# One PSUM bank per feed-forward slice, and a new order of all steps, in an RWKV-7 and SwiGLU kernel

## The chip, the cores and the metric

The kernel runs on one core of a Trainium2 chip. The metric is device time in microseconds (us) of one execution. Before the change three runs took 1074.79, 1076.04 and 1078.73 us; the median is 1076.04 us. A core has five engines with queues of their own: TensorE (PE, with its weight loads shown apart as PEld), VectorE (DVE), ScalarE (ACT), GpSimd (POOL) and SyncE (SP, which issues DMAs here). An engine takes its instructions strictly in the order of its queue, and waits between engines are made with semaphores.

## What is computed

The first half is the RWKV-7 recurrence for 4 batches of 8 heads, 768 steps, head size 40. The second half is a SwiGLU feed-forward block on the 3072 x 320 result.

```python
for t in range(S):
    y[:, :, t] = einsum('bhd,bhde->bhe', r_t, state)
    Sa = einsum('bhde,bhe->bhd', state, a_t)
    state = state * w_t[:, :, None, :] - einsum('bhd,bhe->bhde', Sa, b_t)
    state = state + einsum('bhd,bhe->bhde', v_t, k_t)
...
xn = x / sqrt(mean(x * x) + 1e-6) * rms_g      # x: (3072, 320)
g = xn @ w_gate                                # (320, 1536)
out = (g * sigmoid(g) * (xn @ w_val)) @ w_out  # (1536, 320)
```

## The kernel before, in words

**Stages.** The sequence is cut into 24 chunks of 32 steps. For every chunk, `front` loads the inputs and builds the matrices of the chunk (transposes, "gramk" products, their scaled copies), `inverse` inverts a triangular matrix by small DVE steps (`early_inverse` for the first four chunks), and `main` carries the state over, forms the chunk's output and normalises it into `xg`. After every second chunk `feed(g)` (L941) runs the feed-forward block on 256 token columns: 12 groups in all. In the first group the weights are also narrowed (L975) and written to DRAM as twelve slices `sW[f]`, which later groups load again.

**A feed-forward pair.** `feed` takes the twelve slices of 128 hidden units two at a time, so a pair has the slices e = 0 and e = 1, and there are 72 pairs. A pair takes one PSUM room `hh` of 128 x 2 x 512 f32 (L952), that is two banks. Its steps are:

- `h64` (L959): four matmuls with 64 rows, for the last 64 of the 320 model dimensions; gate and value of both slices,
- `h` for each e (L962): four matmuls of 128 x 256 columns, two for the gate and two for the value,
- `act` (L964): ACT computes the SiLU of the gate into `sg`,
- `tt` (L965): DVE multiplies the value with it into `hT`,
- `out` (L966): two matmuls of 128 x 320 add `hT` times the output weights into `po`.

Before the change, bank 0 of the room holds the two gates and bank 1 the two values, so either slice lies half in each bank (L953).

**Rooms and pairs.** Eight PSUM banks are used: `po` has two, and three tiles `ps` of two banks each, called pairs, hold everything else. A room (transposes, products, levels, feed-forward pairs: 499 in all) is given one of the three pairs by the string `PAIRS`.

**Order.** No loop decides in which order the engines work. `Plan.add` records every step with what it reads and writes, and `Plan.issue` then emits all 6028 recorded steps in the order that the string `ORDER` gives (each number is an offset from the first step not yet emitted; "-" emits a warm-up matmul into `po`, L1017, 151 of them). Semaphore waits are not in that string. They are derived by the framework as the steps are emitted, from the tiles which each step touches.

The level step of `main` (L882 to L885) and the step `down` (L887 to L895), which also shares a room between several users, come up in the prediction: a room `yl` (L914) takes three levels, two in bank 0 and one in bank 1, and DVE adds each of them into `y`.

Of the kernel before, what the change touches and what calls it, by code (L numbers as in the profile page):

```python
# [17 lines left out]
P = 128  # L18
# [15 lines left out]
85 84 76 83 58 78 73 86 74 59 60 75 5 89 61 88 53 77 80 4 43 6 201 7 87 90 44 8 334 62 9 - - - - - - - - 93 10 18 79  # L34
11 12 214 557 13 213 567 14 15 94 566 210 16 17 95 558 108 200 - - - 97 96 19 335 20 21 2 209 22 23 98 25 199 568 26
100 578 202 24 101 107 569 111 57 - - - - - 102 106 124 589 27 122 112 392 109 103 52 119 113 104 54 577 155 125 110
204 105 120 - - - - - - 114 203 117 121 559 211 598 118 46 131 129 132 45 562 560 212 597 563 588 561 394 123 115 136
586 384 133 134 - - - - - 126 130 116 47 564 3 145 383 135 336 128 137 48 144 143 141 587 219 142 51 570 127 565 146
138 337 55 573 1005 216 579 281 393 220 582 608 571 390 234 379 239 607 572 583 580 380 251 574 222 38 221 609 575 581
42 - - - - - - - - 223 82 226 339 91 64 227 338 39 81 139 224 263 576 238 153 56 249 247 590 206 584 228 382 237 591  # L40
272 593 40 233 232 585 381 154 148 594 33 140 205 229 592 389 235 250 28 248 - - 325 236 32 245 36 230 147 260 282 391
246 259 150 35 34 326 595 0 36 270 155 214 148 242 243 62 605 598 230 - 239 40 616 599 601 628 64 49 91 600 602 30 48
626 1135 28 257 603 29 241 68 150 255 65 0 1347 194 0 194 84 173 0 - - - 182 540 200 0 557 184 1 186 935 542 540 0 506
515 527 257 513 300 0 111 97 110 61 112 96 51 439 458 122 50 243 480 0 244 0 58 255 242 0 259 709 104 120 246 708 247
456 470 258 488 719 0 256 470 457 242 0 716 265 487 104 0 268 0 0 265 473 0 262 277 0 273 0 236 0 260 0 269 0 461 241
- - - - - - - 237 242 0 0 278 242 243 252 0 252 0 0 89 0 99 246 0 97 0 230 94 440 0 230 94 440 231 - - - - - - - - -
240 441 244 0 0 468 440 451 255 0 42 468 269 469 258 215 440 239 204 0 0 257 253 203 93 449 92 212 0 235 - - - - - - -
- 246 0 437 0 262 0 246 247 436 245 464 470 258 259 469 260 244 - - 255 471 465 468 466 0 215 466 269 256 445 697 255
478 686 93 94 264 95 687 270 96 266 97 0 97 470 695 2 98 99 3 100 471 101 473 1 102 0 468 99 470 100 471 101 441 102
103 258 104 105 260 106 - - - - - - - - - - - 0 504 106 107 473 108 0 108 502 0 108 109 469 110 111 0 0 0 0 0 - - 13 0  # L50
374 16 146 143 14 147 142 15 13 355 - - - 25 386 358 0 358 386 388 16 387 389 25 390 79 17 391 28 70 147 355 191 69
356 80 148 149 26 359 0 28 2 29 149 0 149 150 29 0 149 31 185 391 23 32 390 29 150 356 151 186 33 389 0 151 29 387 152
27 40 187 153 154 155 156 33 157 158 159 160 161 34 162 36 163 164 37 165 41 391 38 42 392 39 394 561 166 395 393 552
0 42 548 395 209 0 560 165 42 395 548 210 43 428 211 427 557 44 - - - 565 166 558 45 167 549 168 0 566 168 739 565 567
738 571 169 579 - - 45 728 572 0 124 139 0 535 682 0 535 545 140 578 536 141 0 547 545 546 543 578 0 558 554 567 0 519
- - - - - - 517 377 696 378 380 381 695 518 120 685 135 526 - - - - - - 522 686 379 527 382 136 530 383 554 529 121 -
- 141 540 123 523 565 539 122 537 142 125 538 124 524 - - - - 145 525 148 534 149 152 154 551 535 147 555 - - 157 146
# [3 lines left out]
607 367 478 34 568 - - 35 830 594 36 567 820 38 - 476 37 571 366 570 0 605 356 433 434 435 436 120 437 0 317 318 319  # L61
320 441 321 322 323 324 355 456 458 459 442 4 357 325 457 326 327 328 443 0 443 328 329 330 331 357 0 35 331 3 0 37
450 359 3 36 358 331 332 357 333 356 0 462 448 330 461 464 331 332 468 364 447 463 31 467 476 458 333 365 334 335 0
425 439 441 302 426 436 0 6 439 2 0 435 332 2 436 443 444 0 448 332 442 334 443 333 340 449 0 297 329 342 32 330 - 3
33 341 334 0 332 331 0 332 293 441 295 333 0 438 0 436 333 336 295 337 309 438 338 1 375 342 310 365 374 515 27 292 0
362 292 26 28 44 339 29 34 27 32 338 0 646 29 34 336 647 32 0 439 64 315 647 339 440 634 441 63 340 0 287 413 606 312
313 607 623 12 314 615 414 0 410 310 411 603 619 27 412 475 413 620 414 415 621 416 311 633 28 417 812 418 312 625 - -
- - 476 313 419 420 421 822 258 314 422 423 0 810 423 625 637 477 2 0 819 2 257 0 420 421 645 310 422 0 - - - - - 310
422 3 313 32 630 311 423 33 643 424 641 631 312 0 0 637 20 635 420 647 613 21 421 611 648 819 23 38 22 422 809 423 39
659 24 3 612 36 818 424 651 25 808 621 425 59 660 426 249 427 58 0 427 3 25 428 249 4 28 47 0 - 614 428 429 28 430 431  # L70
0 26 25 614 617 484 31 27 627 0 458 590 400 600 401 0 12 582 32 401 33 583 25 0 579 30 21 - - - - - - - - - 588 29 591
22 453 397 428 398 605 23 0 23 429 24 609 0 590 24 397 588 602 1 604 398 601 429 430 399 2 427 0 584 - - - - - - - - -
- - - - - 4 397 0 25 397 4 0 393 394 28 21 23 27 395 598 24 22 424 607 0 35 395 37 396 24 2 424 47 397 398 38 399 400
# [4 lines left out]
976 716 416 663 729 634 977 562 563 717 713 986 665 564 565 566 975 567 401 568 714 569 985 570 571 967 572 723 722 -  # L78
0 403 726 402 572 401 573 0 726 738 736 573 739 574 664 575 737 576 577 3 723 751 578 579 760 580 747 581 582 633 583
4 584 0 584 585 634 586 636 587 635 588 734 633 0 746 588 - - - - - 403 757 589 722 590 3 404 591 592 593 594 595 596  # L80
# [290 lines left out]
def kernel(  # L371
# [36 lines left out]
    DM = H * D  # L408
# [9 lines left out]
    GT = CG * P  # L418
# [74 lines left out]
    def pe(kind, steps, more=[]):  # L493
        def issue(at):
            for s in steps:
                s[3](at)
        plan.add("PE", kind, issue, [s[0] for s in steps] + more, [x for s in steps for x in s[1:3]])
# [58 lines left out]
    for m in range(4):  # L556
        e = eye[m * BH:(m + 1) * BH]
# [492 lines left out]
```

## Time and profile before

| what | us |
|---|---|
| runs | 1074.79, 1076.04, 1078.73 |
| span of the profiled execution | 1078.2 |
| PE busy | 1010.2 |
| DVE busy | 834.2 |
| ACT busy | 462.2 |
| POOL busy | 309.0 |

The results give no time for the profiled execution beside its span; the span is 2.2 us over the median of the runs and 0.5 us under the slowest run. The profile lists for each engine how long it was busy and, for groups of equal instructions, how long they took together, how long one took, and how long the engine sat idle right before them and what ended that wait. PE writes each f32 matmul as two records, so a group of 1152 records is 576 matmuls.

### The profile page before, as it was taken

How to read it: one execution, taken by the hardware profiler on the slowest of the kernel's cores; microseconds unless marked ns; L12 is line 12 of the kernel's file. 1: busy time of each engine (PE TensorE's matmuls, PEld its weight loads, DVE VectorE, ACT ScalarE, POOL GpSimd, SP SyncE). 2: the span in 40 equal slices, each digit the busy share in tenths (PEclk: the TensorE clock that was granted, in tenths of full speed). 3: DMA queues.
4: the chain of work that ended last, by engine and by line, in shares of the span. 5: the costliest groups of instructions: out<-in, count | busy, mean ns of one | idle time of the engine just before them, and what ended most of it. 6: DMA issues, size and time to landing. Idle time of an engine off the chain costs nothing. (4 is left out here: it accounts for less than half of the span.)

```text
span 1078.2 us, 53465 instructions
## 1 busy us (share of the span) xinstructions
PE 1010.2 (94%) x23406; PEld 828.3 (77%) x23406; DVE 834.2 (77%) x2861; ACT 462.2 (43%) x1043; POOL 309.0 (29%) x554
## 2 busy tenths in 40 slices
PE   6767899999999999999999999998999999999998
PEld 6766778777888787877788778887777887887776
DVE  7887879876868888887897888887788889797420
ACT  6845756643543433532443434433344344342211
POOL 9714404120532223241331331331332331200000
PEclk9778999999999999999999999999999999999999
DMA  9965448766564364574465654665545553744242
GB/s 180 196 155 123 73 106 220 213 127 177 124 142 122 99 150 116 144 145 120 96 152 133 146 126 112 142 142 123 126 106 110 134 150 90 162 109 123 77 140 86
DMA packets 172456, 143.34 MB, mean 133 GB/s; under 512 B 125504, under 2 KB 143872, under 8 KB 172224
## 3 DMA queue, kind: packets, MB, share of 16 engines
q1 hardware_dynamic: 153856, 116.96, 42.4%
q0 software_dynamic: 16192, 22.64, 12.2%
q8 instruction: 184, 3.01, 1.2%
q10 hardware_dynamic: 2176, 0.33, 0.2%
q14 instruction: 48, 0.39, 0.1%
HBM read 123.86 MB, written 15.99 MB: 130 GB/s over the span
## 5 line engine op out<-in xcount | busy, mean ns | idle before, releaser
L488 PE MATMUL ps<-xg,wf 128*128 128x256 f32 (+1 forms) x1728 | 355.2, 392 | 4.7 <-DVE xg L446 1.1
L488 PEld LDWEIGHTS ps<-xg,wf 128*128 128x128 f32 (+1 forms) x1728 | 261.6, 189 | 60.4 <-issue 16.9
L488 PE MATMUL po<-wf,hT 128*128 128x320 f32 x576 | 180.1, 445 | 0.1
L446 DVE TENSOR_TENSOR tmp<-Yi,M 128x60 f32<-128x60 f32 (+24 forms) x620 | 129.5, 209 | 19.7 <-DMA M<-sB 6.9
L446 DVE TENSOR_TENSOR Yi<-Yi,tmp 128x60 f32<-128x60 f32 (+24 forms) x620 | 130.2, 210 | 12.7 <-DVE ss L446 0.2
L466 ACT ACTIVATE sg<-ps 128x256 f32<-128x256 f32 x144 | 52.4, 383 | 192.4 <-PE ps L488 182.7
L488 PEld LDWEIGHTS po<-wf,hT 128*128 128x128 f32 x576 | 102.6, 191 | 34.0 <-issue 1.7
L485 POOL DMA_DIRECT2D VU<-in_v_dram x92 | 53.6, 587 | 234.2 <-PE ps L488 157.0
L446 DVE TENSOR_TENSOR hT<-ps,sg 128x256 f32<-128x256 f32 x144 | 59.0, 419 | 62.4 <-ACT sg L466 55.9
L469 ACT COPY KN<-ps 128x640 f32<-128x640 f32 x96 | 66.2, 691 | 76.6 <-PE ps L491 27.9
L488 PEld LDWEIGHTS ps<-Ab,K 40*64 40x64 f32 x4608 | 78.3, 139 | 26.4 <-issue 8.5
L446 DVE TENSOR_TENSOR K<-K,T 128x512 f32<-128x512 f32 (+1 forms) x192 | 93.3, 495 | 4.2 <-ACT K L469 2.1
L488 PE MATMUL ps<-Ab,K 40*64 40x56 f32 x4608 | 88.0, 225 | 8.8 <-ACT K L469 3.7
L485 POOL DMA_DIRECT2D kbn<-in_b_dram x92 | 53.4, 584 | 147.9 <-PE ps L488 147.0
L446 DVE TENSOR_TENSOR As<-ps,msi 128x256 f32<-128x256 f32 (+1 forms) x186 | 79.2, 475 | 18.3 <-PE ps L488 17.4
L469 ACT COPY K<-K 128x256 f32<-128x256 f32 (+1 forms) x168 | 71.8, 443 | 41.3 <-PE ps L488 20.3
L488 PEld LDWEIGHTS ps<-As,KN 128*40 128x40 f32 x3072 | 64.6, 122 | 15.1 <-issue 9.7
L485 POOL DMA_DIRECT2D wn<-in_w_dram x92 | 51.6, 565 | 83.7 <-DVE KN L446 34.7
L485 POOL DMA_DIRECT2D kbn<-in_k_dram x92 | 53.5, 585 | 73.8 <-PE ps L488 73.5
L488 PE MATMUL ps<-As,KN 128*40 128x32 f32 x3072 | 71.1, 203 | 3.7 <-issue 2.7
L446 DVE TENSOR_TENSOR y<-y,ps 128x256 f32<-128x256 f32 x119 | 49.9, 419 | 19.7 <-PE ps L488 17.6
L446 DVE COPY_PREDICATED LT<-near,ps 128x384 f32<-128x384 uint32 (+2 forms) x72 | 52.3, 727 | 3.6 <-PE ps L488 1.9
(133 smaller groups left out, 1544.5 us busy)
## 6 DMA issues: line engine op xcount, KB each, us to landing
wf<-sW SPq DMA_DIRECT2D x144, 480.0 KB, 4.3
M<-sB SPq DMA_DIRECT2D x80, 128.0 KB, 3.8
rn<-in_r_dram SPq DMA_DIRECT2D x24, 160.0 KB, 4.5
sW<-ex SPq DMA_DIRECT2D x16, 240.0 KB, 4.3
out_dram<-o SPq DMA_DIRECT2D x48, 80.0 KB, 3.9
kbn<-in_k_dram POOLq DMA_DIRECT2D x92, 40.0 KB, 3.5
kbn<-in_b_dram POOLq DMA_DIRECT2D x92, 40.0 KB, 3.3
wan<-in_a_dram POOLq DMA_DIRECT2D x46, 80.0 KB, 4.7
```

Of the source, the lines that this page charges most:

```text
L446: plan.add("DVE", kind, lambda at: fn(at(o), *m(at)), [o], aps(*args))
L466: plan.add("ACT", "act", lambda at: nc.scalar.activation(at(o), at(a), f, **kw), [o] + aps(acc), [a])
L469: plan.add("ACT", "copy", lambda at: nc.scalar.copy(at(o), at(a)), [o], [a])
L485: plan.add(by, "dma", lambda at: queue.dma_start(out=o, in_=i), [o], [i])
L488: return o, lhsT, rhs, lambda at: nc.tensor.matmul(at(o), lhsT, rhs, start=start, stop=stop, skip_group_check=True)
```

## The change

Three things change.

1. The room of a pair is cut the other way: slice e takes bank e, with its gate in the first 256 columns and its value in the last 256.
2. The four `h64` matmuls come gate first. The two that stand next to each other are now the two slices' gates (rows 0 to 63 and 64 to 127), then the two values. The 64-row weights are stored to fit: the slice with even f holds the last 64 rows of both gates, that with odd f those of both values.
3. `ORDER` and `PAIRS` are new strings. Both have the same steps, the same 151 warm-up matmuls, and 499 rooms; 43 rooms have another pair.

```diff
 ORDER = """
-85 84 76 83 58 78 73 86 74 59 60 75 5 89 61 88 53 77 80 4 43 6 201 7 87 90 44 8 334 62 9 - - - - - - - - 93 10 18 79
...
 PAIRS = """
-0120112210001221022012220120200102100112221210100202110000202212201000111120112120200021220001012222000200201102100111
...
+1202112110002121221112020120200102020212220210100202110000212212201010101120112110200021220001012222000200201102100111
...
             hh, sgs, hTs = plan.room(), sg_.next(), hT_.next()
-            h = [hh[:, :, e * GT:(e + 1) * GT] for e in range(2)]
+            h = [hh[:, e].rearrange("p (q t) -> p q t", q=2) for e in range(2)]
...
-            pe("h64", [mm(h[e][:, q], wk[e][4][half(q)], x[half(q), 2, :], e == 0, False) for e in range(2) for q in range(2)],
+            pe("h64", [mm(h[e][:, q], wk[q][4][half(e)], x[half(e), 2, :], q == 0, False) for q in range(2) for e in range(2)],
                [hh])
...
-            (lambda t: t[half(0), DM - cut + 2 * P:], moe_w_gate[last, f0:f1], "raw64"),
-            (lambda t: t[half(1), DM - cut + 2 * P:], moe_w_val[last, f0:f1], "raw64")])
+            *((lambda t, i=i: t[half(i), DM - cut + 2 * P:], (moe_w_val if f % 2 else moe_w_gate)[last, (f // 2 * 2 + i) * P:(f // 2 * 2 + i + 1) * P],
+               "raw64") for i in range(2))])
```

Engine by engine the new order is a near neighbour of the old one. Of the 905 PE steps 400 keep their place, and the mean move is one place; the 2858 DVE steps move by 7.5 places on average, the 1024 ACT steps by 3.9, the 545 POOL steps by 7.1 and the 696 SP steps by 5.7.

More of the change, by code (lines that the diff above doesn't have):

```diff
@@ L33 @@
 ORDER = """
-85 84 76 83 58 78 73 86 74 59 60 75 5 89 61 88 53 77 80 4 43 6 201 7 87 90 44 8 334 62 9 - - - - - - - - 93 10 18 79
[L35 to L57, printed above, removed]
[3 rows of a table removed]
-607 367 478 34 568 - - 35 830 594 36 567 820 38 - 476 37 571 366 570 0 605 356 433 434 435 436 120 437 0 317 318 319
@@ L62 @@
[L62 to L71, printed above, removed]
@@ L72 @@
-22 453 397 428 398 605 23 0 23 429 24 609 0 590 24 397 588 602 1 604 398 601 429 430 399 2 427 0 584 - - - - - - - - -
-- - - - - 4 397 0 25 397 4 0 393 394 28 21 23 27 395 598 24 22 424 607 0 35 395 37 396 24 2 424 47 397 398 38 399 400
[4 rows of a table removed]
-976 716 416 663 729 634 977 562 563 717 713 986 665 564 565 566 975 567 401 568 714 569 985 570 571 967 572 723 722 -
-0 403 726 402 572 401 573 0 726 738 736 573 739 574 664 575 737 576 577 3 723 751 578 579 760 580 747 581 582 633 583
-4 584 0 584 585 634 586 636 587 635 588 734 633 0 746 588 - - - - - 403 757 589 722 590 3 404 591 592 593 594 595 596
[147 rows of a table removed]
+84 73 83 74 86 85 88 78 77 76 87 75 392 5 58 43 27 4 44 214 53 - 577 578 558 569 557 566 6 7 8 18 9 10 11 12 93 94 13
@@ new lines @@
+14 15 16 17 19 20 21 23 25 24 22 95 108 26 100 113 101 125 - 97 98 107 96 111 106 112 109 567 0 567 78 392 203 44 37
+58 382 46 210 199 211 47 208 89 80 334 0 332 586 595 587 584 87 585 89 80 60 208 58 200 197 199 32 59 211 153 52 68
+201 40 33 31 64 30 65 53 154 - - - - - 100 - - - - 101 108 577 578 122 557 558 117 119 120 132 118 102 116 103 121 560
+112 - 113 115 135 561 - - - - - - - - 568 114 128 127 133 571 569 129 570 134 559 131 572 562 78 563 90 596 - 130 573
+- 124 126 140 125 139 - 217 - - - 218 232 580 220 219 334 136 - - 237 142 224 141 143 221 - 337 579 335 336 222 137
@@ new lines @@
+249 225 581 235 582 236 - 151 - - 226 - 588 138 231 246 589 590 152 148 605 616 145 574 1 583 146 147 604 627 606 607
+615 149 150 - - - - - 323 - - 261 144 377 388 29 378 380 61 38 387 55 49 204 62 379 382 67 203 389 392 44 48 230 97
+247 591 233 214 26 206 39 205 234 245 270 227 592 228 241 229 242 - 238 243 248 257 597 324 600 253 240 255 244 256
+601 239 593 258 - - 269 608 598 260 609 610 254 259 - 250 611 - 397 266 - - - - - - 251 612 399 398 - - - - - 262 - -
+- 252 400 599 264 268 155 613 156 265 157 404 158 412 159 405 160 602 161 417 162 163 1004 635 594 1003 267 277 - -
@@ new lines @@
+401 617 278 402 411 263 - - 406 - 164 165 166 416 603 625 0 619 245 599 247 246 597 244 620 140 141 142 143 144 145
+146 147 148 149 150 151 152 402 153 414 154 155 156 157 158 388 383 387 386 395 380 398 381 382 400 391 - 601 401 393
+397 396 591 592 399 413 411 394 593 408 392 594 406 595 412 159 248 587 249 - - - - - 403 - - - 160 609 42 252 253 7
+20 1 188 189 27 23 36 10 327 161 849 840 407 196 254 602 405 419 409 603 621 255 404 256 423 257 258 624 420 418 604
+410 259 - - - - - - - 415 - - 163 165 164 162 596 629 628 630 631 416 260 605 261 262 606 421 263 430 431 622 623 -
@@ new lines @@
+166 167 168 169 - 298 632 633 422 417 301 299 302 300 1107 634 359 839 358 43 8 303 304 850 39 369 368 186 0 168 169
+163 160 343 161 162 375 376 377 47 48 0 360 0 0 0 0 0 356 0 0 0 0 0 0 0 358 0 358 0 0 357 0 0 146 147 0 0 150 360 151
+0 357 358 191 30 28 - 151 152 360 153 154 38 36 155 33 156 157 158 159 342 386 385 34 35 39 361 192 194 - 29 41 - 160
+161 162 163 164 165 353 0 30 386 31 - 39 0 41 360 393 392 395 373 394 46 0 3 1 0 161 86 557 32 42 162 163 164 165 166
+39 385 167 40 44 41 386 168 169 45 46 47 48 49 - 0 65 549 561 560 559 552 567 - 732 565 556 562 566 550 551 210 - 570
@@ new lines @@
+569 381 382 1093 391 568 392 0 0 - 46 0 0 139 344 0 140 - - 524 532 525 344 136 118 345 536 0 118 119 141 120 345 534
+536 334 522 578 0 137 0 138 119 518 519 528 527 530 - 142 - 523 143 146 148 543 545 524 525 531 160 544 526 - 147 - -
+535 151 149 154 538 150 333 377 376 537 156 158 - - 344 120 378 0 541 378 539 120 - - 545 535 154 160 151 557 538 553
+152 165 158 161 162 163 0 676 575 695 687 690 691 20 120 686 684 553 550 555 539 551 2 0 0 154 622 156 370 539 371 540
+369 372 157 158 545 159 623 625 624 536 538 537 548 556 549 160 161 550 - 687 688 553 669 114 115 112 113 685 679 670
@@ new lines @@
+10 671 672 680 0 560 442 441 443 444 446 445 574 573 435 0 45 - - 438 46 12 - 435 0 573 46 47 827 574 576 577 12 493
+48 - - 0 - 14 - 577 15 0 0 0 0 0 0 309 0 446 309 354 355 447 451 312 452 313 314 438 699 691 698 315 464 316 317 318
+445 319 320 442 450 321 322 323 324 0 324 475 325 326 327 442 298 328 459 329 356 448 447 460 0 0 454 1 2 355 460 357
+358 455 359 441 328 459 329 3 456 356 0 30 111 32 33 31 849 850 446 364 448 326 327 328 329 330 449 331 447 467 462
+461 332 333 458 463 468 464 473 476 365 334 34 459 37 38 475 474 335 0 - 435 6 436 0 0 0 432 420 328 - - - 447 330 329
@@ new lines @@
+448 296 442 441 439 440 3 331 332 340 339 4 341 426 5 32 33 0 28 29 30 327 328 331 329 336 330 0 331 336 30 337 31 - 0
+308 0 336 437 436 435 0 287 433 43 34 33 440 441 307 29 31 32 64 30 63 442 443 444 415 428 445 0 445 511 446 447 448
+338 337 335 336 176 642 643 177 187 287 449 339 450 340 341 342 451 652 0 255 254 27 256 257 30 7 0 2 0 618 619 307
+617 324 150 334 615 325 610 611 335 599 601 609 608 600 614 819 598 809 820 810 - 279 - 280 29 0 - - 471 306 - 621 414
+622 629 0 414 415 416 0 416 417 418 386 305 306 28 419 252 470 - - - 307 472 26 27 253 308 309 3 - 8 310 616 4 - 420
@@ new lines @@
+421 631 630 29 422 632 423 424 425 30 617 311 9 312 313 5 32 0 27 25 57 58 35 38 37 47 615 248 638 650 634 420 421 422
+423 424 612 636 425 426 427 428 4 0 615 618 428 616 27 634 619 636 646 28 58 248 622 30 645 621 29 631 632 31 617 429
+- 0 - 0 - 456 594 596 3 13 434 - - - - - - - - - - 435 438 6 437 436 27 7 8 616 28 625 0 397 28 398 597 29 399 400 401
+594 402 403 404 405 8 609 9 596 32 0 25 23 24 4 430 5 9 431 26 601 6 600 27 10 595 447 28 597 - 20 615 604 396 0 396
+28 29 612 397 597 10 6 398 399 400 595 433 20 0 25 34 26 36 37 46 599 601 27 - 0 0 0 370 0 367 406 402 404 403 368 572
@@ new lines @@
+401 574 369 2 392 575 399 400 0 0 573 404 367 402 368 369 405 407 585 - - - 4 586 578 14 577 579 25 370 390 0 392 -
[3 rows of a table added]
+727 566 567 568 569 570 571 741 728 753 715 713 773 714 401 - 663 0 - 4 0 4 402 738 401 400 633 0 569 570 571 572 573
+574 734 759 575 576 577 578 579 580 581 582 736 0 582 583 584 585 586 587 588 589 3 590 591 662 592 634 632 635 633
+719 - - 0 399 - 400 404 401 405 589 590 591 714 592 593 594 595 596 597 598 717 718 406 402 0 624 709 724 725 729 0
+726 597 709 710 711 720 741 721 598 599 738 725 735 722 737 742 - 401 405 407 418 428 417 732 733 600 601 602 739 603
[159 rows of a table added]
@@ L228 @@
 """
 PAIRS = """
-0120112210001221022012220120200102100112221210100202110000202212201000111120112120200021220001012222000200201102100111
-0112202000011221102122212200211202022022000011000020220020011122112120010011221011122210001020022121001222220200121010
-1220202110022021220021221222111210110202012021121000002020222101010111121000120212220000221022212022101110012021110002
-0020222022211000002121122111200011110200001202211022020010021211001202102001102012021011201220022100102222202110211111
-012000001002222222210120120
+1202112110002121221112020120200102020212220210100202110000212212201010101120112110200021220001012222000200201102100111
@@ L236 @@
+0112202000011221102122212200201202022022000011000020220020011112112120010011221011122210001020022121001222220200121010
+1220202112022021220021221202111210110102012021121000001020222101010111121000120212220000221022202022101110000022110002
+0020222022211000002121122111200011110200002202201022010010021211001202102001102012021011201220002000102222212110211111
+010001001002220222110102102
 """
```

316 rows, old and new, of the table ORDER are left out of this document.

## The prediction

> **What bounds the kernel now.** I read the page's head first, then a table of two stretches, then the waits of PE, then the timeline of the end.
>
> ```profile
> span 1078.2 us, 53465 instructions
> PE 1010.2 (94%) x23406; PEld 828.3 (77%) x23406; DVE 834.2 (77%) x2861; ACT 462.2 (43%) x1043; POOL 309.0 (29%) x554
> PE   6767899999999999999999999998999999999998
> PEclk9778999999999999999999999999999999999999
> ```
>
> TensorE (PE) is the bound from the fifth slice on; before, DVE (7 to 9 tenths), the loads and a lowered clock share the time. The table of stretches (start:end, length, then busy time and records of PE, PEld, DVE, ACT, POOL, clock, DMA share, GB/s) puts numbers on it:
>
> ```profile
> 150.00:1014.00 864.00, 834.64 (x19714) 678.93 (x19713) 700.26 (x2456) 357.15 (x819) 232.87 (x398) 1.00 0.56 135
> 1014.00:1078.00 64.00, 58.93 (x522) 45.35 (x514) 14.82 (x37) 8.45 (x23) 0.55 (x1) 0.99 0.32 98
> ```
>
> In the body PE is idle for 864.0 - 834.6 = 29.4 us. The waits of PE in that stretch (us in total, times, longest) say on whom:
>
> ```profile
> PE ps L488 <- issue: 13.6, 21, 1.8
> PE ps L491 <- DMA kbn<-in_k_dram: 2.1, 3, 1.1
> PE ps L491 <- DVE T L446: 1.5, 1, 1.5
> PE ps L488 <- DMA LT<-sY: 1.3, 1, 1.3
> PE ps L488 <- DVE xg L446: 1.1, 2, 0.7
> ```
>
> About half is "issue", which no order of other engines' work removes. All PE waits on ACT and DVE in that answer add up to about 8 us, those on DMAs to 4.5. **So a better order can gain some 13 us in the body at most**, while a stall of PE that is added there costs its full length, unless it takes the place of one of these.
>
> **The change, part by part.**
>
> *The matmuls.* The steps are the same in number and shape: per pair four h64, eight h, four out. h stays at 277.0 us for 1152 records (0.24 each), out at 180.1 for 576 (0.31), h64 at 80.8 for 576 (0.14). h64 records cost little over half of an h record, so two neighbours with 64 rows each run side by side. After the change the neighbours are the slices' gates, again in different row halves and different banks. I take 0; if they lost their overlap it would be up to 576 x (0.24 - 0.14) = 58 us. That the two neighbours differ in rows and in banks before and after excludes it for me. The weights' 64-row blocks are stored by the same two loads of 64 x 128 from other columns: 0.
>
> *DMAs and queues.* SP and POOL keep every step; they move by 5.7 and 7.1 places on average. The sW loads land 4.3 us (median) after issue. In the built order, the PE work standing between what a load waited for and the matmul that uses it is at least 5.1 us before (SP) and 4.3 after, and at least 7.4 and 5.5 on POOL; 11 SP loads have less than 7 us on both sides. That work hides them: 0, between -2 and +2 us.
>
> *The waits.* This is the part that counts. I compared the two built programs, with their semaphore waits, on each engine. The intent of the layout is that slice 1's h may write bank 1 while ACT and DVE still read slice 0 in bank 0. **The built program does not do that.** Its waits are by whole tile, and a pair's tile is both banks: where SiLU and product of one slice are emitted ahead of the other slice's h, that h still waits for them. The new order puts it right there, as if it were free. Six times an h with a wait on DVE stands directly behind the other h of its pair; before, this never happens. In the last feed group alone there are four.
>
> To count all such places I worked out a cover for each PE instruction that waits for ACT or DVE: the PE work (records times the busy time per record of its row) that stands between the last matmul the awaited instruction depends on and the waiting matmul. Beyond the first 60 us of PE work:
>
> | cover under 0.5 us | before | after |
> |---|---|---|
> | reader of the other bank of the same tile | 0 | 13 |
> | same bank, or data | 1 | 10 |
>
> The 13 are ten h and three level steps. The other ten are mostly new too; some hang on the same rule at one remove (a SiLU that waits for the other slice's h).
>
> *The price of one.* The end of the timeline (start, length) shows the chain without anything in between: SiLU, product, then the next weight load of PE.
>
> ```profile
> 1033.24 3.32 PEld L488 LDWEIGHTS ps<-xg,wf 128*128 128x128 f32 x16 [0.33 <-issue]
> ...
> 1037.00 0.39 ACT L466 ACTIVATE sg<-ps 128x256 f32<-128x256 f32 x1 [4.02 <-PE ps L488]
> 1037.42 0.42 DVE L446 TENSOR_TENSOR hT<-ps,sg 128x256 f32<-128x256 f32 x1 [5.66 <-ACT sg L466]
> ...
> 1037.95 0.84 PEld L488 LDWEIGHTS po<-wf,hT 128*128 128x128 f32 x4 [0.33 <-DVE hT L446]
> ```
>
> The last h weights are in at 1033.24 + 3.32 = 1036.56 and its stream (0.24) is over at about 1036.8; PE goes on at 1037.95. So an uncovered h waits 1.15 us at most, and 0.95 by SiLU start alone; I take 1.1. One operation of ACT or DVE (0.38 to 0.42, with about 0.25 of handing over in this chain) is 0.65.
>
> - nine h behind SiLU and product: 9 x 1.1 = 9.9
> - one h behind a SiLU alone: 0.65
> - three level steps behind one DVE addition: 3 x 0.65 = 1.95
> - ten others: 7 x 0.65, and three with covers of 0.31 to 0.47, together 0.8: 5.3
> - the one of before: -0.65
>
> Sum +17.2 us. It could be as little as 0.5 each, 22 x 0.5 = 11, or, if ACT and DVE are held up by older work (DVE is busy 81% of the body), 1.3 each, 22 x 1.3 = 29.
>
> *What is given back.* A PE stall lets ACT, DVE and loads catch up, so some of the 8 + 4.5 us of PE's old waits in the body vanish: I take -4, between 0 and -13. In the tail nothing is given back; PE there waits only for such chains, and the four uncovered h of the last group cost 4.4 us right on the end. Other gains of the new order: the covers show none (below 1.0 us in the whole stretch: 9 instructions before, 28 after), I take -2. The first 60 us, where 7 covers are under 0.5 against 3, and the warm-up matmuls stand scattered instead of in blocks: 0, between -6 and +8.
>
> Sum: 17.2 - 4 - 2 = +11 to +12 us on a span of 1078.2. The span stood 2.2 over the median of the runs, so the median 1076.0 becomes **1088 us**, 1.1% slower.
>
> **A rule against the trace.** Nothing in the trace of before shows PE writing one bank of a tile while the other is read, since its waits keep that out. The Trainium skill, "PSUM — Partial Sum Buffer", section "PSUM bank collisions raise a hardware error", says that each bank of a partition is a memory of its own and that only accesses to the same bank collide. By that rule the hardware would allow what the new order wants; it is the program's waits that don't.
>
> **The rivals.**
>
> *It gains (other side).* If the awaited instructions are over before PE arrives at the 13 places on the other bank, the order's intent comes true: 17.2 - 12.5 = 4.7 us of stalls stay, 2 come back, and if half of the 13 us of idle body time is won, 1076 + 4.7 - 2 - 6.5 = 1072; with the other ten hidden as well, 1067. It decides at a cover of about 1.1 us per place (0.65 for one operation); the built order shows 0. For it speaks only that PE's idle time in the body leaves something to win. Chance of a time under 1070.7 us: 0.09.
>
> *The stalls are absorbed.* Each added stall pays for one that would come later: the waits of 1.8 us "issue" and 1.1 us on loads then hide behind it. Up to 13 of 17 us: 1076 + 4 = 1080. Against it: the tail's 4.4 us have nothing to hide in. Within 0.5%: 0.16.
>
> *The start loses its clock.* PEclk is 0.7 to 0.8 in the second to fourth slice, where PE idles in longer pieces; blocks of warm-ups that are now singles could add one or two such stretches. A stretch of 10 us at half clock costs 5 us: 1088 + 10 = 1098. It is part of the slower cases, 0.12.
>
> *The layout alone does nothing.* It holds in my forecast already; without the new order's places the time would be 1076.
>
> **How the numbers follow.** The forecast 1088 has 0.63, the slow start 0.12, together 0.75 for slower by over 0.5%, which is about what a measurement of this kernel can tell from no change; 0.16 for within it; 0.09 for faster. Low end: 11 us of stalls with 10 given back, 1077. High end: 29 of stalls with 4 given back and 3 lost at the start, 1104.
>
> **What would show it.** Right: PE's idle time in the body grows from 29 to about 40 us; among PE's waits, "ps from DVE hT" and "ps from DVE y", 0.4 and 0.2 us before, rise to about 8 and 2 us; the stretch of the last feed group is about 4 us longer; busy time per record of h, h64 and out stays. Wrong: h64 per record far over 0.14; PE's waits on hT unchanged; a body shorter than before; or the difference made in the first 150 us.

## The result and the profile after

The changed kernel takes 1129.06 us (median of 4 runs, 1123.16 to 1136.54) against 1076.92 us (4 runs, 1074.79 to 1078.73): ratio 1.0471 [1.0404, 1.0538]. It is 52 us slower, where 11 to 12 us were forecast, and the time lies above the range. The profiled execution took 1133.23 us and has a span of 1131.1 us, 52.9 us more than that of before.

The head of the page of the changed kernel, then its slices of PE and of the granted clock:

```profile
span 1131.1 us, 53443 instructions
...
PE 1024.4 (91%) x23406; PEld 835.4 (74%) x23406; DVE 835.3 (74%) x2861; ACT 458.1 (40%) x1043; POOL 315.1 (28%) x554
...
PE   6777999899899999999998989899899998899987
...
PEclk9987899999889999999998989999999999999999
```

PE is the only engine that the 53 us can be read from. It is busy 14.2 us longer with the same 23406 records, and idle 1131.1 - 1024.4 = 106.7 us instead of 68.0: 38.7 us more. The extra busy time is about what the clock would make: its mean went from 0.980 to 0.967, and 1010.2 x (0.980 / 0.967 - 1) is 13.6 us, an estimate. From the eighth slice on the PE row has nine 8s, where it had two; three of them (slices 11, 22 and 24) stand over an 8 in the clock's row. The others are idle time at a clock of 9 tenths or more. Busy time per record of the parts that the layout touches is what it was: h 277.5 us for 1152 records (277.0 before), out 180.5 for 576 (180.1), h64 84.1 for 576 (80.8).

The table of stretches of the changed kernel (columns as in the prediction), cut so that the last one is again 64 us long:

```profile
150.00:1067.00 917.00, 851.73 (x19829) 689.83 (x19828) 707.77 (x2471) 355.42 (x825) 236.57 (x401) 0.98 0.51 128
1067.00:1131.00 64.00, 54.80 (x394) 40.40 (x392) 11.23 (x28) 7.83 (x20) 0.55 (x1) 1.00 0.30 97
```

In the body PE is idle 917.0 - 851.7 = 65.3 us, where it was 29.4; in the last 64 us 9.2, where it was 5.1. The first 150 us hold 3186 PE records (3187 before) and 117.9 us of PE work (116.6): as the traces stand, the loss isn't there.

The waits of PE in the body, as before (us in total, times, longest):

```profile
PE ps L502 <- issue: 12.4, 13, 3.3
PE ps L502 <- DVE hT L460: 10.3, 10, 1.9
PE ps L502 <- DVE LT L460: 6.6, 2, 4.8
PE ps L502 <- DVE y L460: 6.5, 8, 2.0
```

Over the whole run PE waits 18.6 us on the product hT, where it waited 0.6. That is the wait that the prediction counted. But LT, a small product of the recurrence, now stops PE for 4.8 us in one piece, and the new layout has nothing to do with LT. The list of the waits of all engines shows why. DVE itself is stopped, and so is ACT; first the changed kernel, then before:

```profile
ACT sg L480 <- PE ps L502: 241.4, 84, 7.8
...
DVE hT L460 <- ACT sg L480: 78.3, 42, 6.8
...
DVE hT L460 <- PE ps L502: 19.6, 4, 11.5
```

```profile
ACT sg L466 <- PE ps L488: 182.7, 77, 9.0
...
DVE hT L446 <- ACT sg L466: 55.9, 34, 7.3
...
DVE hT L446 <- PE ps L488: 5.5, 1, 5.5
```

A reader (ACT's SiLU or DVE's product) that waits for PE although its own slice is done waits for the other slice's matmuls. Matched record by record with the built program, all four products in the changed kernel's row do so. Of their 19.6 us they are held for 10.1 us by the other slice alone, that is, past the moment at which their own inputs were there and DVE was free; before, it was one product with 2.5 us. **Most of the held readers are SiLUs on ACT:** 20 of them, for 43.8 us counted in the same way, where before had 11 with 19.0 us. A late SiLU shows up on DVE as a wait on `sg`. All this is idle time of engines that are not the bound, so it says that readers are held, and not yet what that costs PE.

One of them, in time. The chain of waits of the changed kernel between 284 and 300 us (start, length, what):

```profile
291.04 0.70 ACT KN L483
...
291.78 3.09 PE ps L502 x72
...
294.97 0.06 DVE hT L460
...
295.37 0.83 DVE KN L460
296.19 0.60 DVE K L460
...
297.24 0.73 DVE LT L460
...
297.99 0.73 DVE LT L460
...
298.74 0.74 DVE LT L460
...
299.61 0.39 PE ps L502 x9
```

The product of slice 1 in a pair of the second feed group has its inputs, and waits until PE has written the h of slice 0 at 294.9: 4.4 us. Behind it in DVE's queue stand KN, K and three LT, which take DVE until 299.5, and PE's next matmul needs the last LT. PE runs out of other work and waits its 4.8 us on "LT". The stretches around it:

```profile
280.00:290.00 10.00, 9.94 (x180) 7.76 (x179) 8.28 (x33) 6.35 (x16) 4.24 (x8) 1.00 0.65 187
290.00:300.00 10.00, 5.19 (x170) 4.27 (x172) 5.50 (x14) 3.76 (x9) 0.59 (x1) 0.94 0.03 6
300.00:310.00 10.00, 10.00 (x294) 8.38 (x287) 6.13 (x20) 4.85 (x12) 1.23 (x2) 0.72 0.30 68
310.00:320.00 10.00, 8.64 (x130) 6.91 (x126) 2.79 (x13) 1.38 (x2) 9.77 (x17) 0.66 0.50 103
```

PE is half idle from 290 to 300, and then works 20 us at a clock of 0.72 and 0.66. The Trainium skill, "TensorE: Matmul & The Clock Gate", section "Why this matters for your kernels", warns of gaps of PE of more than about 3 us, after which the clock falls to half; the row of 290 to 300 with the one behind it agrees. How much of the low clock belongs to this pause stays open: in a repeat of the changed kernel (`h1_change_again`) the same pause of 4.8 us comes with 0.82, 0.84 and 1.00 in these three stretches, and in `h2_one_pair_again`, where the pause is gone, the clock is 1.00, 0.83 and 0.88.

The end, from the timeline of PE's weight loads in the last feed group of the changed kernel (start, length, idle before and what ended it):

```profile
1080.36 1.59 PEld L502 LDWEIGHTS ps<-xg,wf 128*128 128x128 f32 x8 [0.33 <-issue]
1083.29 1.59 PEld L502 LDWEIGHTS ps<-xg,wf 128*128 128x128 f32 x8 [1.33 <-DVE hT L460]
...
1088.27 1.75 PEld L502 LDWEIGHTS ps<-xg,wf 128*128 128x128 f32 x8
1091.35 1.59 PEld L502 LDWEIGHTS ps<-xg,wf 128*128 128x128 f32 x8 [1.33 <-DVE hT L460]
...
1099.01 1.59 PEld L502 LDWEIGHTS ps<-xg,wf 128*128 128x128 f32 x8 [2.00 <-ACT sg L480]
```

Where the wait is 1.33 or 2.00, the eight weight loads are a slice's h that directly follows the other h of its pair and waits for that other slice's SiLU and product; a fourth such place (1.39) follows at 1108.2. PE itself is idle there for 0.93, 0.93, 1.63 and 0.99 us, 4.5 us together. From the last chunk's normalisation to the last copy of the output, before took 44.2 us and the change 50.0.

### The profile page after: what moved, and what is told of

Same layout as the page of the kernel before. It is cut to its first block, busy times and chain, and to the rows that moved or that the text cites. A ratio compares the mean times of both kernels' runs of the same rounds, so it can differ in the third digit from the quotient of the medians.

```text
span 1131.1 us, 53443 instructions
## 1 busy us (share of the span) xinstructions
PE 1024.4 (91%) x23406; PEld 835.4 (74%) x23406; DVE 835.3 (74%) x2861; ACT 458.1 (40%) x1043; POOL 315.1 (28%) x554
## 4 chain that ended last, share of the span: by engine, by line
PE 59%; DVE 16%; DMA 8%; issue 6%; ACT 5%; POOL 3%; SPq 2%; DVEq 0%; ACTq 0%; POOLq 0%
PE ps L502 38%; PE po L502 10%; PE ps L505 9%; DVE tmp L460 2%; SPq L499 2%; DVE LT L460 2%; PE po L1031 2%; DVE K L460 2%; DVE Yi L460 2%; DMA kbn<-in_b_dram 2%; POOL kbn L499 2%; DVE y L460 2%; DVE As L460 2%; DVE hT L460 1%; DMA M<-sB 1%
## 5 line engine op out<-in xcount | busy, mean ns | idle before, releaser
L502 PE MATMUL ps<-xg,wf 128*128 128x256 f32 (+1 forms) x1728 | 359.2, 396 | 16.2 <-DVE hT L460 13.9
L502 PE MATMUL po<-wf,hT 128*128 128x320 f32 x576 | 180.5, 445 | 1.2 <-DVE hT L460 1.2
L483 ACT COPY K<-K 128x256 f32<-128x256 f32 (+1 forms) x168 | 72.6, 445 | 31.6 <-DVE K L460 15.9
L489 POOL TENSOR_TENSOR ss<-ss,mhalf 128x1 f32<-128x1 f32 x24 | 18.6, 776 | 147.1 <-DVE ss L460 146.9
```

What stands on the lines that cost most here:

```text
L483: plan.add("ACT", "copy", lambda at: nc.scalar.copy(at(o), at(a)), [o], [a])
L489: plan.add("POOL", "tt", lambda at: nc.gpsimd.tensor_tensor(o, a, b, op), [o], [a, b])
L502: return o, lhsT, rhs, lambda at: nc.tensor.matmul(at(o), lhsT, rhs, start=start, stop=stop, skip_group_check=True)
```

## The experiments

The main theory was the prediction's, held to the result: the layout costs nothing; the new order was planned as if waits went by bank, the program's waits go by tile, and that difference is the loss, direct (PE waits) and at one remove (DVE and ACT held). Rivals: the layout itself costs, the new order is slow for reasons of its own (start, queues, other engines), or a few bad places make the whole loss.

Ratios are against the kernel before, timed on the same chip as the run. Its median there was between 1074.19 and 1081.87 us.

### The two halves

`e1_layout_alone` is the changed kernel with the two strings of before; `e2_order_alone` is the kernel before with the two new strings, so its slices still lie half in each bank.

```diff
 # e1: after.py
-ORDER, PAIRS = (after's)
+ORDER, PAIRS = (before's)
 # e2: before.py
-ORDER, PAIRS = (before's)
+ORDER, PAIRS = (after's)
```

> The new layout (one bank per slice, h64 gates first, weights stored to fit) with the old order and pairs. Theory A (the loss comes from the new order, whose steps wait for readers of the other bank because waits are made by whole tile): same as before, 1077 us within 0.5%, since the waits of the built program are nearly those of before. Theory B (the layout itself costs, say by gate and value streaming into one bank): a good part of the 52 us, over 1090. Busy time per h64 record stays 0.14 by A.

> The new order and pairs with the old layout. Theory A: as slow as the whole change, 1120 to 1137 us, because by whole tile the built program has the same waits under either layout (23 places with under 0.5 us of cover, as in the change). Theory B: near before, under 1090. If waits were really lifted by the layout anywhere, this one would be slower than the whole change.

Measured: layout alone 1082.02 against 1081.87 us, 0.9999 [0.9954, 1.0044]; order alone 1140.49, 1.0534 [1.0466, 1.0602]. **The whole loss comes with the order, and the layout does nothing under either order that these intervals show.** PE's waits of the order alone look like those of the change:

```profile
PE ps L502 <- DVE hT L460: 19.1, 16, 2.0
PE ps L502 <- issue: 14.8, 19, 1.7
PE ps L502 <- DVE y L460: 8.3, 9, 1.9
PE ps L502 <- DVE LT L460: 7.2, 3, 4.8
```

That the slices share no bank in the change, and share both here, makes no difference that the intervals of the two ratios (1.0471 and 1.0534) tell apart: the waits go by the tile.

### Waits by bank

Can the order be fast if the waits follow its intent? `e3_waits_by_bank` notes for every emitted instruction which banks of its pair it touches, and tells the framework that two instructions of different engines on different banks, with no other tensor in common that one of them writes, need no wait between them. `e4_before_by_bank` has the same in the kernel before.

```diff
+    def apart(self, p, pair, done, touched):
...
+        for room, old, ins, banks in past:
+            q = self.pieces[old]
+            if q.engine != p.engine and not (q.writes & (p.reads | p.writes) or q.reads & p.writes):
+                for i, b in mine:
+                    if not b & banks:
+                        self.tc.declare_no_dep(i.ins, ins, reason="other bank")
```

Here `p` is the step that would wait, `q` an earlier one in the same or the previous room of the pair.

> The whole change, with the framework told for each two instructions of different engines on different banks of a tile that share no other tensor that they need no wait; everything else as in the change. 4 places with under 0.5 us of cover are left instead of 23. Theory A: most of the 52 us goes, 1065 to 1085 us. Theory C (the new order is slow by itself, in its start or its tighter covers): little goes, 1105 or more.

> The kernel before, with the same lifting of waits between different banks. Its order leaves over 1 us of PE work at nearly every wait, so by theory A there is little to win: 1070 to 1078 us. If it gains much more (under 1065), waits by tile were already a main cost before the change.

Measured: e3 1086.77 us, 1.0047 [1.0006, 1.0089]; e4 1074.75, 0.9928 [0.9887, 0.9969], both against 1081.87. The same steps in the same order on every engine lose 4.7% with waits by tile and about 0.5% with waits by bank. The head of e3's page:

```profile
span 1086.2 us, 53428 instructions
...
PE 1017.9 (94%) x23406; PEld 834.3 (77%) x23406; DVE 834.7 (77%) x2861; ACT 460.1 (42%) x1043; POOL 315.2 (29%) x554
```

PE is idle 68.3 us there, as before the change (68.0), and PE's waits on hT and y, and the product's waits on PE, are gone from its list. Waits by bank are also what the hardware allows. In e3's trace 57 reads by ACT and DVE overlap in time with a matmul that writes the other bank of the same tile, in those of before and of the change none. This agrees with the rule that the prediction cites from the Trainium skill, "PSUM — Partial Sum Buffer", section "PSUM bank collisions raise a hardware error".

A small debt stays. By bank the new order is still about 1.2% slower than the old one (1.0047 against 0.9928). The clock may be part of it. The bodies of e3 and then e4:

```profile
150.00:1022.00 872.00, 839.19 (x19735) 682.06 (x19734) 702.09 (x2459) 354.47 (x816) 234.71 (x400) 0.98 0.55 134
150.00:1006.00 856.00, 830.74 (x19708) 677.83 (x19700) 699.68 (x2457) 355.64 (x821) 233.20 (x398) 1.00 0.56 136
```

e3 has the change's clock of 0.98 in its body, although the waits are gone and no pause of PE there is longer than 2.1 us; e4 and before have 1.00. So in these profiles the lower clock goes with the new order, and they do not show it to come from the waits by tile. What lifting them gives back is PE's idle time: 38.4 of the 38.7 us, while PE stays busy 7.7 us longer than before.

### Which waits

Four variants of e3 lift a part of the waits only. Each adds one condition to the test in `apart`:

```diff
 # f1: only PE is let go on past ACT and DVE
+            if p.engine == "PE" and ...
 # f2: only ACT and DVE are let go on past PE
+            if q.engine == "PE" and ...
 # f3: only in the last feed group
+            if p.key[:2] == q.key[:2] == ("feed", 11) and ...
 # f4: only in the pair of the 4.8 us wait (second feed group, fifth pair)
+            if p.room == q.room and p.key[:2] == ("feed", 1) and 44 <= p.key[2] < 55 and ...
```

> The whole change, with only those waits lifted in which PE would wait for ACT or DVE that read the other bank. Places with under 0.5 us of cover go from 23 to 10. Theory D (PE's own stalls at the uncovered places are the loss, each with its knock-on): most goes, to 1085 to 1100 us. Theory E (the loss is mostly ACT and DVE held up in their queues by waits on PE's writes to the other bank): PE's own 19 us or so come back, 1105 to 1115.

> The whole change, with only those waits lifted in which ACT or DVE would wait for PE that writes the other bank. By theory D little goes, 1120 or more; by theory E the larger part, 1090 to 1112 us.

> The whole change, with the waits between different banks lifted in the last feed group alone, where no other stage runs beside it and queues hold nothing else. Both theories: the stretch behind the last chunk gets 4 to 6 us shorter (four uncovered h of 1.1 us), so 0.4 to 0.5% under the change.

> The whole change, with the waits between different banks lifted in one single pair of the 72, the fifth of the second feed group. There the DVE product of one slice stands idle for 4.4 us until PE has written the other slice, and seven DVE steps of the next chunks queue behind it. If the price of a place is the chain of SiLU and product alone, 1 us goes, which can't be seen. Theory E: up to the 15 us that the change loses between 284 and 333 us go, so 1108 to 1120 us.

| lifted | us, before 1074.19 | ratio |
|---|---|---|
| f1: PE's waits for readers of the other bank | 1114.34 | 1.0323 [1.0241, 1.0406] |
| f2: readers' waits for PE's writes to the other bank | 1105.18 | 1.0280 [1.0235, 1.0324] |
| f3: both, last feed group | 1129.68 | 1.0489 [1.0424, 1.0554] |
| f4: both, one pair | 1125.21 | 1.0467 [1.0417, 1.0516] |

In us of a 1076 us kernel, from 1.0471: lifting PE's waits returns 15.9, lifting the readers' waits 20.6, lifting both (e3) 45.6, that is 9 more than the two together. Each of these ratios has an interval of 4 to 9 us to either side, and they come from different chips, so neither the difference of the two parts nor the 9 us is clear of the noise. **The readers' waits are worth about as much as PE's own, and of them the prediction counted only what reached a PE instruction within half a microsecond.** The lists of waits of f1 and then f2 show that each leaves the other half in place:

```profile
DVE hT L494 <- PE ps L536: 18.0, 4, 9.9
...
PE ps L536 <- DVE LT L494: 7.8, 3, 4.8
```

```profile
PE ps L536 <- DVE hT L494: 15.1, 11, 2.2
```

With PE free (f1) DVE is still held 18 us and PE still waits 7.8 us on LT. With the readers free (f2) the wait of the product on PE isn't in the list any more, LT falls to 1.6 us over two lines, and PE's own 15.1 us on hT stay.

f3's last stretch is 44.3 us, as before the change, against 50.0 in the change, e2, f2 and f4; f1 has 44.3 too, so the tail's 5.7 us are PE's direct waits. The total of f3 does not show 5.7 us (0.5%): the intervals of f3 and the change overlap. In f4 PE's waits on LT fall from 7.8 to 3.1 us, and none is longer than 1.8: the wait of 4.8 us was the held product's doing. The stretch from the fifth to the sixth chunk, 33.8 us before and 49.1 in the change, is 40.2, 9 us shorter. But f3, in which this pair is as in the change, has 45.0 there, so not all of the 9 us need be the pair's; f4's total doesn't show them either (more below).

### Which rooms and which engines

```diff
 # g1: PE against ACT and DVE, both ways; waits between ACT and DVE stay
+            if "PE" in (p.engine, q.engine) and ...
 # g2: only inside a feed-forward pair's room
+            if p.key[0] == "feed" and p.room == q.room and ...
 # g3: everywhere else
+            if not (p.key[0] == "feed" and p.room == q.room) and ...
```

> The whole change with the waits between PE and the readers of the other bank lifted both ways, but those between ACT and DVE that read different banks kept. If the two kinds lifted singly (15 and 21 us) only add up, 1093 to 1098; if they work on each other, all that the lifting of everything gave, 1078 to 1088. A slower result would say that ACT and DVE waiting for each other costs as well.

> The whole change with all waits between different banks lifted inside the rooms of feed-forward pairs alone. 7 places with under 0.5 us of cover are left of 23. If the loss is that of the slices' own bank plan: 1085 to 1098 us.

> The whole change with those waits lifted in all other rooms (levels, state, transposes) and between rooms, and kept inside the pairs' rooms. 20 places are left. If the pairs carry the loss: 1110 to 1130 us, otherwise under 1100.

Against 1081.07 us: g1 1082.92, 1.0033 [0.9994, 1.0072]; g2 1086.98, 1.0057 [1.0010, 1.0104]; g3 1130.58, 1.0464 [1.0404, 1.0524]. g1 and g2 stand where e3 stands, g3 where the change stands. **So the loss sits in the rooms of the feed-forward pairs, between PE and the two readers.** Waits between ACT and DVE, and the rooms of the recurrence (the three level steps of the forecast among them), are worth nothing that these runs can tell.

### The price of one place

Two kernels put such places into the kernel before, with its own layout and rooms. In `g4_eight_places`, at eight pairs, SiLU and product of one slice are emitted ahead of the other slice's h, so that PE waits for them uncovered; seven of the eight products also move up by 3 to 9 DVE steps, and four SiLUs by 1 to 4 ACT steps. In `h3_eight_held`, at eight other pairs, the other slice's h is emitted ahead of the product, so that DVE's product waits for PE; the instructions of all five engines stand in the same order as before, and only the waits differ. One place of each:

```diff
 # g4
-565 712 564 3 563 404 8 0 3 639 0 403 3 0 400
+565 712 564 0 0 1 561 402 6 2 638 403 3 0 400
 # h3
-295 333 0 438 0 436 333 336 295 337 309 438 338 1 375 342 310 365
+295 333 0 438 334 310 2 0 436 336 295 337 438 338 375 342 310 365
```

> The kernel before, old layout and old order, but at eight pairs outside the last feed group SiLU and product of the slice whose h comes first are put ahead of the other slice's h, which stood right behind the first, so that it waits for them with nothing in between: eight places of cover 0 and nothing else. At 1.1 us each: 1086 us, 0.8% over before. If a place in the body costs twice that, by the DVE and ACT work that is late behind it: 1093 to 1100 us. If PE's stall is given back later: 1077 to 1081.

> The kernel before with every engine's queue exactly as before; only the emission is changed at eight pairs, so that the DVE product of one slice waits for the other slice's h (on PE's writes to a tile that it shares) instead of that h waiting for the product. Theory E, a DVE instruction that is held holds all of DVE behind it and PE a little later: 1.5 to 3 us a place, 1088 to 1102 us. If held DVE steps are covered by DVE's idle share of a fifth: 1076 to 1082.

g4: 1099.29 against 1081.07 us, 1.0173 [1.0123, 1.0224], 18.2 us or 2.3 a place. h3: 1108.24 against 1078.51, 1.0271 [1.0215, 1.0327], 29.7 us or 3.7 a place. The waits that belong to it, first of g4:

```profile
PE ps L488 <- DVE hT L446: 14.2, 8, 2.9
```

PE's eight waits last 1.8 us each, 13.8 us more than before. But PE's idle time in g4's profile is 73.8 us, 5.8 more than before: 8 us of the waits are given back elsewhere. PE is also busy 7.9 us longer, at a clock of 0.974. And of h3:

```profile
DVE hT L446 <- PE ps L488: 38.6, 9, 6.6
PE ps L488 <- DVE LT L446: 5.8, 3, 3.3
PE ps L488 <- DVE hT L446: 3.6, 2, 1.8
```

The product's waits on PE are 33.1 us longer than before, eight times 4.1; counted as above, past its own inputs, 27.8 us, eight times 3.5. PE is idle 82.0 us, 14 more than before, on LT, hT and others that come late from DVE's queue, and busy 10.2 us more at a clock of 0.970. **The place with the held product is the dearer of the two, though its wait stands on DVE and not on PE: everything behind the product on DVE comes late, and PE waits for that.** This is by the place: each product is also held about twice as long as PE waits in g4, so by the microsecond of waiting it is not the dearer one.

### Again, and the other combination

`h1_change_again` is the changed kernel, `h2_one_pair_again` is f4, on one chip, to see whether the 9 us of one pair reach the total. `h4_layout_by_bank` is the changed layout with the old strings and all waits by bank.

> The whole change once more, to stand beside the single pair on the same chip: 4.7% over before by every theory.

> The whole change with the waits lifted in the one pair of the second feed group, more rounds. In its first look the stretch between the fifth and sixth chunk was 5 to 9 us shorter than in the change and the total did not show it. If that is real, 5 to 9 us under the change on the same chip (0.5 to 0.8%); if the time comes back as a wait further on, no difference.

> The new layout with the old order and pairs, and waits lifted between different banks: the layout with the waits it was made for, in an order that does not lean on them. At least as fast as the old layout with the same lifting (0.7% under before), as a slice's reads no longer share a bank with the other slice's writes: 0.985 to 0.993 of before.

Against 1078.51 us: h1 1131.80, 1.0481 [1.0431, 1.0531]; h2 1129.01, 1.0455 [1.0406, 1.0503]; h4 1073.31, 0.9932 [0.9893, 0.9971]. The change repeats. The one pair is inconclusive a second time: 2.8 us, inside both intervals. Its stretch is 46.6 us in h1 and 42.3 in h2, so that only 4.3 us were there to be seen. h4 equals e4: with waits by bank, too, the layout is worth nothing as long as the order isn't made for it. No run has the new order with waits by bank under the old layout, so what the layout is worth there stays open. e4 and h4 are the fastest kernels of this study, 0.7% below the kernel before and 5% below the change.

## Why the prediction was wrong

**Layout, h64, DMAs: right.** Forecast 0; the layout alone gave 0.9999, and busy time per record is the same within 0.3% for h and out and 4% higher for h64 (0.146 against 0.140 us, 3 us in all). No wait on a load is among PE's four longest in the body.

**The mechanism: right.** The waits go by whole tile and the new order puts instructions where only waits by bank would let them pass. Lifting those waits in the feed rooms returns nearly all (g2). The direction was right for that reason, and the rival that gains fell with it.

**The direct price: about right, a little small.** The sum of PE's added stalls was 17.2 us. On hT PE waits 18.0 us more, and 6.9 us more on y (forecast 1.95 for three level steps). The level steps' part is of little account in the total: g2 keeps 3.9 us of waits on y where g1 has 0.4, and their ratios don't differ. By f1, lifting PE's waits alone returns 15.9 us. In the tail 4.4 us were forecast, 5.8 came: three of the four places cost what the row of before said (weight loads idle 1.33, 1.33 and 1.39 us, where it gave 1036.56 to 1037.95, 1.39 us), and the fourth 2.0. PE's own idle time at the four is 4.5 us.

**The held readers: the term that failed.** "Ten others: 7 x 0.65, and three with covers of 0.31 to 0.47, together 0.8: 5.3" was all that the sum had for waits at one remove. The covers were worked out for PE instructions only, so a DVE product that waits for the other slice's h counted when it made a PE instruction late within half a microsecond, and for nothing otherwise. But in DVE's queue KN, K and LT stand behind it. A SiLU that is held on ACT was likewise left out. f2 returns 20.6 us for the readers' waits alone, and h3 prices a held product at 3.7 us. The prediction named DVE's 81% in the body, and used it only to lift the price of one place from 1.1 to 1.3; the right use was to list what stands behind each held instruction of DVE and ACT, and to count their waits with PE's.

**"What is given back" did not come.** The sum took -4 us, since a stall of PE lets the others catch up, and -2 for other gains of the new order. Where only PE is stopped the first is right: in g4 13.8 us of added waits become 5.8 us of idle time. In the change PE's added waits on hT and y, 24.9 us, go with 38.7 us more idle time. Here DVE and ACT are held too, and PE waits for what is late behind them.

**The clock** was in the forecast only as the rival of the start (10 us); here it fell in the body. The 13.6 us that it makes of the 52.9 us of the profiled execution are not shown to follow from the waits, since e3 without them has 0.98 in the body too. Why the clock is lower with the new order stays open.

**Term by term**, in us of a 1076 us kernel: forecast 12.5 for PE's uncovered places, 5.3 for the others, -0.65 for the one of before and -6 given back, 11 to 12 in all. Measured 15.9 (f1), 20.6 (f2), 9 more when both are lifted together, which is within the noise, and 5 that stay in e3: 50.7 by the ratio. The clock's part is inside these figures.

**What stays open.** Why the new order is about 1.2% slower than the old one even by bank: its clock in e3's profile is 0.968 against 0.979 in e4's, and four of its covers are under 0.5 us against one, but no run separates these from the start: up to the fifth chunk's normalisation the profiles of the old order took 278.7 to 281.1 us, those of the new one 276.7 to 290.5. Open too are how the readers' part divides between held products and held SiLUs, and what one pair is worth (f4 and h2), since the 4 to 9 us in its stretch are less than the totals can tell.

## What to carry to other kernels

An order planned by hand or by a planner is only as good as its idea of the waits. Before a finer layout is used to reorder, read from the built program whether the waits are as fine as the layout; here two banks of one tile were one thing to wait for. And count a wait on every engine: a held instruction is priced by what is queued behind it, here 3.7 us for one product on DVE that is held about 4 us, against 2.3 us for an uncovered wait of PE itself of 1.8 us.

## What the runs showed of the hardware

One pause of PE of 4.8 us was followed by 20 us at a granted clock of 0.72 and 0.66, though PE was busy 10.0 and 8.6 of 10 us in them; in the repeat the same pause was followed by 0.84 and 1.00. The clock also falls without such a pause: e3's body has a mean of 0.98 with no pause of PE over 2.1 us. The mean over the whole run does not follow the waits: 0.980 before, 0.967 after and 0.970 with eight held products and no other change, but also 0.968 in e3, whose waits by tile are lifted.

PE can write one bank of a two-bank tile while ACT or DVE reads the other: 57 reads overlap such a matmul in e3, whose ratio is 1.0047 where the change has 1.0471.

The kernel before varied more than its first four runs (0.4% from end to end) let expect: beside e1 to e4 its 25 runs lay between 1072.96 and 1091.71 us, 1.7% apart, and its medians on four chips were 1074.19, 1078.51, 1081.07 and 1081.87 us. Half a per cent could be read only as a ratio on one chip, with its interval.
